# Start of a fused mLSTM and SwiGLU kernel: weight halves on two DMA queues, output gates asked for first, weight block 0 scaled later

## The chip, the cores and the metric

The kernel runs on one NeuronCore of one Trainium2 chip. The metric is the device time of one execution in microseconds (us); lower is better. Beside the plain times there is one profiled execution, whose trace says when each instruction of each engine ran. The engines are PE (matmul, with PEld for its weight loads), DVE (vector), ACT (scalar and activation), POOL (GpSimd) and SP, which only issues DMAs. ACT can issue DMAs too. Each engine works through its own list of instructions in order and waits at an instruction until the semaphores that it names have been raised.

## The reference

First comes an mLSTM cell over 4 batches x 8 heads, 768 steps, head size 40. For each step:

```python
m_new = np.maximum(f_gate[:, :, t] + m, i_gate[:, :, t])
f_stab = np.exp(f_gate[:, :, t] + m - m_new)
i_stab = np.exp(i_gate[:, :, t] - m_new)
C = f_stab * C + i_stab * (v_t outer k_t)
n = f_stab * n + i_stab * k_t
o = 1.0 / (1.0 + np.exp(-o_gate[:, :, t]))
y[:, :, t] = o * (C q_t) / np.maximum(np.abs(n . q_t), 1.0)
```

Its result, seen as x with 3072 tokens and 320 columns (8 heads x 40), goes through a SwiGLU block with 1536 hidden columns:

```python
g = x @ w_gate
val = x @ w_val
out = (g * sigmoid(g) * val) @ w_out
```

q, k, v and the gates are float32. The weights are float64 in memory, so each weight arrives as two 32-bit words.

## The kernel before, in words

The 768 steps are cut into six groups of 128. Group g covers 4 batches x 128 steps, 512 tokens. For each group the cell gives x, a *seam* turns x on PE into xT, and the SwiGLU block runs over 12 blocks m of 128 hidden columns. `hidden(g, m)` does the 10 matmuls gv_ps of both projections (20 in the trace[...]), SiLU on ACT and the product on DVE; `project` multiplies with w_out. While PE does the blocks of group g, the steps of the cell for group g + 1 are put between them by hand in lists called `slots` and `after`. The order on each engine is that of the program text (`manual_schedule`).

Group 0 is special: nothing runs ahead of it. The code from `burn(7)` to `late_sums()` is this start. The cell of group 0 is done in one square of 128 steps, in halves of two batches:

- `first_turn`, `first_scores`, `first_own`, `first_x`: transposes, scores, products and the division that gives x without the output gate.
- `sig(P)`: the sigmoid of the output gates o_sb of half P, on ACT.
- `first_gate(P)`: x times the output gate on DVE; POOL copies 64 columns.
- `first_seam(P, engs)`: 10 transposes on PE in three PSUM tiles (four, four and two transposes), copied to xT by the engines in `engs`; A is ACT, V is DVE.
- `first_state(P, eng)`: the state at the end of the group.
- `burn(n)`: n matmuls on junk data.

Weights come in *pieces*. `PIECES` lists them: pieces 0 and 1 hold one block of w_gate and w_val, pieces 2 to 6 two blocks each, pieces 7 to 9 four blocks of w_out. Piece p from 2 to 6 thus holds blocks 2p - 2 and 2p - 1. A piece of gate and val has two halves, the w_gate half on partitions 0 to 63 and the w_val half on 64 to 127; a half of two blocks is 640 KB. `piece_load(p, home, second)` asks for the w_gate half on SP and for the w_val half on the queue `second` (ACT unless told otherwise). The raw words go into one of two `raw` buffers or into a `home`: piece 2 and later piece 6 lie in h_sb, piece 3 in wo_sb.

A block is then turned from float64 words to float32 in three steps: `scale(j)` on ACT makes `top` and `low` (L184, L186), `join(j)` on DVE puts the top bits together (L193, L194), `rounded(j)` adds `low`, on POOL unless another engine is named (L201). `convert(j)` does all three. In group 0 `hidden(0, m)` converts block m + 2 after its own matmuls and before its own SiLU.

f_sb and i_sb hold the gate rows of the later steps (80 KB each); `late_sums`, `late_maxima`, `late_turns` and `decay` work on them during group 0.

DMAs are told apart by eight semaphores that are dealt out in turn to the DMAs of both queues. A DMA whose semaphore is already in use waits, on the engine that issues it, until the earlier DMA on that semaphore has landed. Whatever stands behind it on that engine waits too.

Of the kernel before, what the change touches and what calls it, by code (L numbers as in the profile page):

```python
# [18 lines left out]
L = 128  # L19
# [5 lines left out]
def kernel(  # L25
# [18 lines left out]
    nc = tc.nc  # L44
# [12 lines left out]
    NKC = DM // HP  # L57
    UH = BH // 2
    UA = UH // 2
    NH = NFC + 1  # L60
# [12 lines left out]
    def flat(t):  # L73
        return t.rearrange("p c t -> p (c t)")

    def bank(name, tag="cell"):
        return psum.tile([128, 512], F32, name=name, tag=tag)
# [4 lines left out]
    def heads(P):  # L82
        return slice(P * UH, (P + 1) * UH)
# [4 lines left out]
    o_sb = const.tile([128, BH, D], F32)  # L88
# [8 lines left out]
    wo_sb = const.tile([128, NFC, DM], F32)  # L97
    h_sb = const.tile([128, NH, TW], F32)
# [7 lines left out]
    f_sb = early.tile([BH, NS - 2, SUB], F32)  # L106
    i_sb = early.tile([BH, NS - 2, SUB], F32)

    def tokens(a, c, P):
        return a[2 * P:2 * P + 2, :, ts(c, L), :].rearrange("b h p d -> p (b h) d")  # L110

    def load(dst, a, c, P):
        nc.sync.dma_start(out=dst[:, heads(P), 0:D], in_=tokens(a, c, P))

    def copy(eng, dst, src):
        if eng is nc.scalar:
            nc.scalar.copy(dst, src)
        else:
            eng.tensor_copy(dst, src)

    def gate_rows(a):
        return a.rearrange("b h s -> (b h) s")

    def spread_rows(a):
        return gate_rows(a)[:, 0:L].unsqueeze(0).to_broadcast([128 // BH, BH, L])

    nc.scalar.dma_start(out=f0, in_=spread_rows(f_gate))
    nc.sync.dma_start(out=i0, in_=spread_rows(i_gate))


    raws = {}
    PIECES = [("gv", 0, 1), ("gv", 1, 1)] + [("gv", m, 2) for m in range(2, NFC, 2)] + [("o", m, 4) for m in range(0, NFC, 4)]

    def piece_load(p, home=None, second=nc.scalar):
        kind, m, n = PIECES[p]
        if kind == "gv":
            a, d = NKC, n * 128
            src = [(slice(i * HP, (i + 1) * HP), w[:, m * 128:(m + n) * 128].rearrange("(c p) f -> p c f", p=HP))
                   for i, w in enumerate((moe_w_gate, moe_w_val))]
            queues = (nc.sync, second)  # L140
        else:
            a, d = n, DM
            src = [(slice(0, 128), moe_w_out[m * 128:(m + n) * 128].rearrange("(a p) d -> p a d", p=128))]
            queues = (nc.sync,)
        if src[0][1].dtype == F32:
            for r, w in src:
                if kind == "o":
                    nc.sync.dma_start(out=wo_sb[r, m:m + n, :], in_=w)
                else:
                    for x in range(n):  # L150
                        nc.sync.dma_start(out=wgv_sb[r, m + x], in_=w[:, :, ts(x, 128)])
            return
        if home is None:
            raw = conv.tile([128, 4 * NKC * 128], U32, name="raw")
        else:
            raw = home.rearrange("p a t -> p (a t)").bitcast(U32)
        raw = raw[:, 0:2 * a * d]
        for (r, w), queue in zip(src, queues):
            queue.dma_start(out=raw[r].rearrange("p (a d) -> p a d", a=a), in_=w.bitcast(U32))
        words = raw.rearrange("p (a d two) -> p a d two", two=2, a=a)  # L160
        raws[p] = (words[:, :, :, 0], words[:, :, :, 1])
        split(p)
# [4 lines left out]
    def split(p):  # L167
        if p in raws:
            lo, hi = raws.pop(p)
            kind, m, n = PIECES[p]  # L170
            if kind == "gv":
                for c in range(n):
                    r = slice(c * 128, (c + 1) * 128)
                    blocks[m + c] = (lo[:, :, r], hi[:, :, r], wgv_sb[:, m + c])
            else:
                for c in range(0, n, 2):
                    blocks[NFC + (m + c) // 2] = (lo[:, c:c + 2], hi[:, c:c + 2], wo_sb[:, m + c:m + c + 2, :])

    def scale(j):
        if j in blocks:  # L180
            lo, hi, dst = blocks[j]
            a, d = hi.shape[1], hi.shape[2]
            top = conv.tile([128, NKC * 128], F32, name="top", bufs=1).rearrange("p (a d) -> p a d", a=a)
            nc.scalar.mul(top, hi.bitcast(F32), 2.0 ** -112)  # L184
            low = conv.tile([128, NKC * 128], I32, name="low").rearrange("p (a d) -> p a d", a=a)
            nc.scalar.mul(low, lo, 2.0 ** -29)  # L186
            blocks[j] = (low, top.bitcast(U32), dst)

    def join(j):
        if j in blocks:  # L190
            lo, top, dst = blocks[j]
            both = dst.bitcast(U32)
            nc.vector.tensor_scalar(both, top, scalar1=3, scalar2=None, op0=ALU.logical_shift_left)  # L193
            nc.vector.scalar_tensor_tensor(both, in0=top, scalar=0x80000000, in1=both, op0=ALU.bitwise_and,  # L194
                                           op1=ALU.bitwise_or)
            blocks[j] = (lo, dst.bitcast(I32))

    def rounded(j, eng=None):
        if j in blocks:
            lo, dst = blocks.pop(j)  # L200
            (eng or nc.gpsimd).tensor_tensor(dst, dst, lo, op=ALU.add)  # L201
# [198 lines left out]
    def xT(n):  # L400
        return xTs[max(n - 1, 0) % 2]
# [32 lines left out]
    def sig(P):  # L434
        nc.scalar.activation(o_sb[:, heads(P)], o_sb[:, heads(P)], AF.Sigmoid)


    def burn(n, tag="cell"):
        t = bank("burn", tag)
        for _ in range(n):  # L440
            nc.tensor.matmul(t, lhsT=junk[:, 0:128], rhs=junk, start=True, stop=True)  # L441
# [4 lines left out]
    A, V, G = nc.scalar, nc.vector, nc.gpsimd  # L446
# [29 lines left out]
    def first_turn(P, src, dst, engs):  # L476
        for b in range(2):
            tp = bank("tp_kq").rearrange("p (a t) -> p a t", t=L)
            for a in range(UA // 2):
                h = P * UH + b * H + 2 * a  # L480
                nc.tensor.transpose(tp[:, a, :], src[:, h:h + 2, :].rearrange("p h d -> p (h d)"), ident)  # L481
            a = P * UA + b * UA // 2
            copy(engs[b], dst[:, a:a + UA // 2, :], tp)
# [20 lines left out]
    def first_x(u):  # L504
        y = first_y.pop(u)
        den = work.tile([128, UH, 1], F32, name="den")[:, 0:H]
        nc.vector.tensor_scalar(den, y[:, :, D:], scalar1=1.0, scalar2=None, op0=ALU.max)
        nc.vector.scalar_tensor_tensor(den, in0=y[:, :, D:], scalar=-1.0, in1=den, op0=ALU.mult, op1=ALU.max)
        nc.vector.reciprocal(den, den)
        nc.vector.tensor_tensor(x_sb[:, u, 0:DM].rearrange("p (h d) -> p h d", d=D), y[:, :, 0:D],  # L510
                                den.to_broadcast([128, H, D]), op=ALU.mult)

    def first_gate(P):
        for u in (2 * P, 2 * P + 1):
            x = x_sb[:, u, 0:DM].rearrange("p (h d) -> p h d", d=D)
            nc.vector.tensor_tensor(x, x, o_sb[:, u * H:(u + 1) * H], op=ALU.mult)
        nc.gpsimd.tensor_copy(x_sb[:, 2 * P:2 * P + 2, DM:], x_sb[:, 2 * P:2 * P + 2, 0:HP])
# [9 lines left out]
    def first_seam(P, engs):  # L527
        for c, eng in zip(range(0, NKC, 2), engs):
            cs = range(c, min(c + 2, NKC))
            tp = bank("tp_x")[:, 0:len(cs) * 2 * L].rearrange("p (c u s) -> p c u s", u=2, s=L)  # L530
            for w in cs:
                for b in range(2):
                    nc.tensor.transpose(tp[:, w - c, b, :], x_sb[:, 2 * P + b, ds(PAIRS[w][0] * HP, 2 * HP)], ident)
            copy(eng, xT(0)[:, c:c + len(cs), 2 * P * L:(2 * P + 2) * L].rearrange("p c (u s) -> p c u s", u=2), tp)
# [13 lines left out]
    first_turn(1, k_sb, kT, (A, A))  # L548
    first_x(0)
    first_turn(1, q_sb, qT, (A, V))  # L550
    piece_load(0)
    load(o_sb, o_gate, 0, 1)
    piece_load(1)
    first_own(1)
    first_values(1)
    first_x(1)
    first_scores(1)
    sig(0)
    nc.scalar.dma_start(out=flat(f_sb), in_=gate_rows(f_gate)[:, L:])
    nc.scalar.dma_start(out=flat(i_sb), in_=gate_rows(i_gate)[:, L:])  # L560
    piece_load(2, h_sb[:, NH - NKC:], nc.sync)
    piece_load(3, wo_sb, nc.sync)
    scale(0)
    sig(1)
    burn(3)
    first_own(2)
    first_own(3)
    first_gate(0)
    first_x(2)
    join(0)  # L570
    first_x(3)
    rounded(0)
    first_gate(1)
    first_seam(0, (A, V, A))
    burn(8, "gen")
    piece_load(4)
    first_seam(1, (V, A, A))
    first_state(0, A)
    convert(1)
    piece_load(5)  # L580
# [222 lines left out]
```

## Time and profile before

| what | value |
|---|---|
| median of 3 runs | 576.04 us (573.17 to 576.25) |
| the profiled execution's own time | 576.29 us |
| its span, first to last instruction | 574.5 us |
| mean granted PE clock | 0.994 |
| moved by DMA | 39.82 MB in 168220 packets |

The profiled execution is 1.8 us longer than its span: that lies before the first and after the last instruction. The page gives the busy time of each engine, then the span in 40 slices. In the slices a digit is the busy share in tenths:

```
PEclk 9989899999999999999999999999999999999999
DMA  9999993396265530355450264360000000000000
```

Each slice is 14.4 us. The granted PE clock dips in the third and the fifth, and the DMA engines are full in the first six.

### The profile page before, as it was taken

The page shows a single profiled execution, that of the slowest core. Times are in us where ns is not written, and L with a number is a line of the kernel's source. Part 1 is how long each engine was busy: PE and PEld are TensorE (multiplying, and loading weights), DVE is VectorE, ACT ScalarE, POOL GpSimd, SP SyncE. Part 2 cuts the span into 40 slices and gives each one's busy share as a digit, 9 for nine tenths or more (in the row PEclk, how much of TensorE's full clock was granted, in tenths as well). Part 3 has the DMA queues.
Part 4 walks back from the last instruction along what each step waited for, and adds up shares of the span by engine and source line. Part 5 has one row for each costly group of instructions (what it writes and reads, how often), then busy time and mean ns, then how long its engine had stood idle before and what let it go on. Part 6 is the DMA issues. An engine that isn't in the chain of part 4 may idle for free.

```text
span 574.5 us, 11872 instructions
## 1 busy us (share of the span) xinstructions
PE 561.7 (98%) x5216; PEld 326.3 (57%) x5218; DVE 219.7 (38%) x378; ACT 143.7 (25%) x224; POOL 107.6 (19%) x104
## 2 busy tenths in 40 slices
PE   9979899999999999999999999999999999999997
PEld 4844545666555566455567455567455567544475
DVE  5656568781335620424630433640333730011100
ACT  4345556433410114210114211024211010111100
POOL 2122425555301132001232001232001110000000
PEclk9989899999999999999999999999999999999999
DMA  9999993396265530355450264360000000000000
GB/s 124 179 208 187 175 264 66 116 167 114 28 68 71 98 57 23 46 60 63 79 86 23 34 71 49 65 111 25 13 2 2 2 2 23 24 1 1 0 24 23
DMA packets 168220, 39.82 MB, mean 69 GB/s; under 512 B 158728, under 2 KB 163336, under 8 KB 168168
## 3 DMA queue, kind: packets, MB, share of 16 engines
q1 hardware_dynamic: 166260, 36.20, 39.5%
q10 hardware_dynamic: 1908, 2.85, 2.6%
q8 instruction: 41, 0.67, 0.5%
q14 instruction: 11, 0.09, 0.0%
HBM read 35.03 MB, written 4.01 MB: 68 GB/s over the span
## 4 chain that ended last, share of the span: by engine, by line
PE 87%; DMA 6%; DVE 3%; ACT 2%; POOL 1%; issue 1%; SPq 0%; ACTq 0%; DVEq 0%; POOLq 0%
PE gv_ps L618 48%; PE o_ps L634 23%; PE o_ps L641 4%; DMA wo_sb<-in_moe_w_val_dram 4%; DMA raw<-in_moe_w_gate_dram 2%; PE intra L370 2%; PE inter L365 2%; PE sp L325 1%; PE add L346 1%; PE tp_x L411 1%; PE burn L441 1%; PE first_y L502 1%; DVE wgv_sb L194 1%; PE tp_kq L481 1%; DVE wgv_sb L193 1%
## 5 line engine op out<-in xcount | busy, mean ns | idle before, releaser
L618 PE MATMUL gv_ps<-xT,wgv_sb 64*128 64x512 f32 x1440 | 321.5, 596 | 3.9 <-POOL wgv_sb L201 3.4
L618 PEld LDWEIGHTS gv_ps<-xT,wgv_sb 64*128 64x128 f32 x1440 | 140.5, 188 | 160.0 <-issue 152.0
L624 DVE TENSOR_TENSOR h_sb<-sg,gv_ps 128x512 f32<-128x512 f32 x72 | 49.5, 687 | 288.3 <-ACT sg L623 273.0
L634 PE MATMUL o_ps<-wo_sb,h_sb 128*128 128x320 f32 x480 | 130.5, 433 | 0.0
L634 PEld LDWEIGHTS o_ps<-wo_sb,h_sb 128*128 128x128 f32 x480 | 90.8, 190 | 38.2 <-issue 0.8
L623 ACT ACTIVATE sg<-gv_ps 128x512 f32<-128x512 f32 x72 | 43.0, 597 | 262.4 <-PE gv_ps L618 262.4
L355 POOL TENSOR_TENSOR C<-C,dec 128x328 f32<-128x328 f32 x20 | 14.5, 737 | 150.3 <-DVE C L357 150.3
L628 ACT COPY z_sb<-o_ps 128x320 f32<-128x320 f32 x24 | 10.2, 426 | 114.1 <-PE o_ps L634 102.7
L428 POOL TENSOR_SCALAR_AFFINE_SELECT w_sb<-w_sb 64x1024 f32<-64x1024 f32 x20 | 28.2, 1408 | 26.1 <-DVE w_sb L423 25.1
L641 PE MATMUL o_ps<-wo_sb,h_sb 128*128 128x320 f32 x96 | 26.9, 437 | 0.0
L391 POOL TENSOR_TENSOR o_sb<-o_sb,y_sb 128x640 f32<-128x640 f32 x10 | 14.2, 1428 | 48.4 <-DVE y_sb L382 48.4
L641 PEld LDWEIGHTS o_ps<-wo_sb,h_sb 128*128 128x128 f32 x96 | 17.9, 190 | 7.2
L201 POOL TENSOR_TENSOR wgv_sb<-wgv_sb,low 128x640 int32<-128x640 int32 x9 | 14.9, 1654 | 33.8 <-DVE wgv_sb L194 30.0
L382 DVE TENSOR_TENSOR y_sb<-y_sb,intra 64x328 f32<-64x328 f32 x40 | 19.7, 493 | 0.9
L335 POOL TENSOR_TENSOR vw_sb<-v_sb,w_sb 128x656 f32<-128x656 f32 x10 | 12.9, 1316 | 31.3 <-issue 29.4
L365 PEld LDWEIGHTS inter<-C,qT 64*64 64x64 f32 x640 | 10.2, 134 | 7.3 <-issue 6.1
L193 DVE TENSOR_SCALAR wgv_sb<-top 128x640 uint32<-128x640 uint32 x12 | 9.0, 746 | 13.0 <-ACT top L184 13.0
L357 DVE TENSOR_TENSOR C<-C,add 128x328 f32<-128x328 f32 x20 | 9.9, 493 | 10.5 <-POOL C L355 10.5
L184 ACT ACTIVATE top<-raw 128x640 f32<-128x640 f32 x12 | 9.6, 799 | 14.1 <-issue 5.3
L423 DVE TENSOR_TENSOR w_sb<-g_T,w_sb 128x1024 f32<-128x1024 f32 x10 | 13.1, 1350 | 0.0
L201 POOL TENSOR_TENSOR wo_sb<-wo_sb,low 128x640 int32<-128x640 int32 x6 | 10.2, 1707 | 15.0 <-DVE wo_sb L194 10.5
L332 DVE TENSOR_TENSOR w_sb<-sp,w_sb 128x512 f32<-128x512 f32 x20 | 12.7, 681 | 0.0
(126 smaller groups left out, 378.3 us busy)
## 6 DMA issues: line engine op xcount, KB each, us to landing
w_sb<-M_dram SPq DMA_DIRECT2D x10, 512.0 KB, 6.4
k_sb<-in_k_dram SPq DMA_DIRECT2D x12, 320.0 KB, 5.7
v_sb<-in_v_dram SPq DMA_DIRECT2D x12, 320.0 KB, 7.2
o_sb<-in_o_gate_dram SPq DMA_DIRECT2D x12, 320.0 KB, 7.0
raw<-in_moe_w_out_dram SPq DMA_DIRECT2D x3, 1280.0 KB, 7.5
out_dram<-z_sb SPq DMA_DIRECT2D x24, 160.0 KB, 1.8
q_sb<-in_q_dram SPq DMA_DIRECT2D x6, 320.0 KB, 8.2
q_sb<-in_q_dram SPq DMA_DIRECT2D x24, 64.0 KB, 2.3
```

The source lines that it names most:

```text
L193: nc.vector.tensor_scalar(both, top, scalar1=3, scalar2=None, op0=ALU.logical_shift_left)
L201: (eng or nc.gpsimd).tensor_tensor(dst, dst, lo, op=ALU.add)
L355: nc.gpsimd.tensor_tensor(state(s + 1)[:, a], state(s)[:, a], dec[:, s - 2, a].unsqueeze(2).to_broadcast([128, UA, D1]), op=ALU.mult)
L365: nc.tensor.matmul(inter[two][half(i), a, :], lhsT=qT[half(two), P * UA + a, half(i)], rhs=state(2 * n + i)[half(two), P * UA + a, :], sta ...
L382: nc.vector.tensor_tensor(t, t, intra[i][half(c)], op=ALU.add)
L391: eng.tensor_tensor(o, o, y[:, :, 0:D], op=ALU.mult)
L428: nc.gpsimd.affine_select(w, w, compare_op=ALU.is_ge, fill=NEG, base=0, pattern=[[0, UH], [1, SUB]], channel_multiplier=-1)
L618: nc.tensor.matmul(ps[i], lhsT=wgv_sb[half(i), m, PAIRS[kc][i], :], rhs=x[half(i), kc, :], start=(kc == 0), stop=(kc == NKC - 1))
L623: nc.scalar.activation(sg, ps[0], AF.Silu)
L624: nc.vector.tensor_tensor(hid(g, m), sg, ps[1], op=ALU.mult)
L634: nc.tensor.matmul(p, lhsT=hid(g, m)[:, ts(u, L)], rhs=wo_sb[:, m, :], start=(m == 0), stop=(m == NFC - 1))
L641: nc.tensor.matmul(ps[u], lhsT=hid(g, m)[:, ts(u, L)], rhs=wo_sb[:, m, :], start=(m == 0), stop=(m == NFC - 1))
```

## The change

Four edits, all in the start of group 0:

1. The requests for f_sb and i_sb move from behind `sig(0)` to the very start, right behind the first gate loads, on ACT.
2. The output gates of half 1 are asked for ahead of piece 0.
3. The val halves of pieces 2 and 3 are asked for on ACT, not on SP; both sigmoids stand ahead of these requests.
4. `scale(0)`, `join(0)` and `rounded(0)` move back. Scaling stands behind ACT's two copies of the first seam, joining behind the gating of half 1 (and behind `piece_load(4)` in the text), rounding behind the copies of the second seam, and on DVE instead of POOL. The third copy of each seam, the small one, goes to DVE and the first two to ACT. The second burn has 6 matmuls instead of 8.

```diff
     nc.sync.dma_start(out=i0, in_=spread_rows(i_gate))
+    nc.scalar.dma_start(out=flat(f_sb), in_=gate_rows(f_gate)[:, L:])
+    nc.scalar.dma_start(out=flat(i_sb), in_=gate_rows(i_gate)[:, L:])
...
-    def piece_load(p, home=None, second=nc.scalar):
+    def piece_load(p, home=None):
...
-            queues = (nc.sync, second)
+            queues = (nc.sync, nc.scalar)
...
     first_turn(1, q_sb, qT, (A, V))
+    load(o_sb, o_gate, 0, 1)
     piece_load(0)
-    load(o_sb, o_gate, 0, 1)
     piece_load(1)
     first_own(1)
     first_values(1)
     first_x(1)
     first_scores(1)
     sig(0)
-    nc.scalar.dma_start(out=flat(f_sb), in_=gate_rows(f_gate)[:, L:])
-    nc.scalar.dma_start(out=flat(i_sb), in_=gate_rows(i_gate)[:, L:])
-    piece_load(2, h_sb[:, NH - NKC:], nc.sync)
-    piece_load(3, wo_sb, nc.sync)
-    scale(0)
     sig(1)
+    piece_load(2, h_sb[:, NH - NKC:])
+    piece_load(3, wo_sb)
     burn(3)
     first_own(2)
     first_own(3)
     first_gate(0)
     first_x(2)
+    first_x(3)
+    first_seam(0, (A, A, V))
+    scale(0)
+    first_gate(1)
+    burn(6, "gen")
+    piece_load(4)
     join(0)
-    first_x(3)
-    rounded(0)
-    first_gate(1)
-    first_seam(0, (A, V, A))
-    burn(8, "gen")
-    piece_load(4)
-    first_seam(1, (V, A, A))
+    first_seam(1, (A, A, V))
+    rounded(0, V)
     first_state(0, A)
     convert(1)
     piece_load(5)
```

Where a line number is given for the changed kernel, the added lines shift it: L184, L186, L193, L194 and L201 become L186, L188, L195, L196 and L203.

## The prediction

> **What bounds the kernel now.** I read the page first, then the windows, then the timelines of PE and ACT, then the chain of waits.
>
> ```profile
> span 574.5 us, 11872 instructions
> ...
> PE 561.7 (98%) x5216; PEld 326.3 (57%) x5218; DVE 219.7 (38%) x378; ACT 143.7 (25%) x224; POOL 107.6 (19%) x104
> ```
>
> TensorE is busy for 98% of the span, so time can come only from where it waits, or from work at a lower clock. The PE timeline (start, length, engine, line, tiles, and in brackets the idle time before) shows where:
>
> ```profile
> 31.99 2.31 PE L533 MATMUL tp_x<-ident,x_sb 128*128 128x128 f32 x10 [2.60 <-DVE x_sb L516]
> ...
> 36.10 4.91 PE L618 MATMUL gv_ps<-xT,wgv_sb 64*128 64x512 f32 x20
> ...
> 43.57 13.15 PE L618 MATMUL gv_ps<-xT,wgv_sb 64*128 64x512 f32 x60 [1.50 <-POOL wgv_sb L201]
> ...
> 59.32 6.50 PE L618 MATMUL gv_ps<-xT,wgv_sb 64*128 64x512 f32 x20 [1.88 <-POOL wgv_sb L201]
> ```
>
> The reader is to see three waits: 2.60 us for gated x, 1.50 for weight block 1, 1.88 for block 4. The last group takes 6.50 us where others take 4.4 (13.15 / 3). The windows say why (columns: stretch, length, busy us of PE, PEld, DVE, ACT and POOL, granted PE clock, DMA share, GB/s):
>
> ```profile
> 36.00:43.00 7.00, 6.00 (x56) 2.79 (x54) 3.50 (x4) 4.02 (x7) 2.07 (x1) 0.99 1.06 207
> 44.00:50.00 6.00, 6.00 (x30) 2.71 (x28) 5.31 (x10) 4.51 (x7) 2.98 (x3) 1.00 1.06 208
> ...
> 60.00:63.45 3.45, 3.45 (x11) 2.71 (x9) 3.42 (x7) 2.10 (x4) 1.55 (x1) 0.51 1.55 141
> ```
>
> After the wait the clock is halved up to 63.45 us. The first two lines show the DMA engines full (share over 1) at 207 and 208 GB/s. Now ACT, in the stretch that leads to block 4:
>
> ```profile
> 40.82 0.61 ACTq L159 DMA_DIRECT2D raw<-in_moe_w_val_dram  x1
> ...
> 52.60 0.73 ACT L279 ACTIVATE keep<-keep 32x640 f32<-32x640 f32 x1 [2.54 <-DVE keep L278]
> 54.77 0.60 ACTq L159 DMA_DIRECT2D h_sb<-in_moe_w_val_dram  x1
> 55.42 0.79 ACT L184 ACTIVATE top<-wo_sb 128x640 f32<-128x640 f32 x1 [2.09 <-DMA raw<-in_moe_w_gate_dram]
> ```
>
> Block 4 belongs to piece 3, whose halves landed at 40.8 and 43.9 (requests at 22.98 and 23.68, 17.8 and 20.2 us to landing). Yet ACT scales it at 55.42. Ahead of it in ACT's order stands the request for piece 6's val half, at 54.77, and this waits for the landing of piece 5's val half, because both use one of eight DMA semaphores: 40.82 + 13.9 = 54.7. From there to PE the chain of waits is fixed:
>
> ```profile
> 55.44 0.77 ACT top L184
> ...
> 57.73 1.54 POOL wgv_sb L201
> 59.28 0.04 issue
> 59.32 6.50 PE gv_ps L618 x20
> ```
>
> So PE's restart at 59.32 is the landing of piece 5's val half (54.7) plus 4.6 us. The page's chain names another transfer there (piece 5's gate half), but that landed at 43.95 + 12.6 = 56.6, after ACT had gone on, so it cannot be the releaser.
>
> [...] 207 GB/s where nearly all packets are SP's (36 to 43 us), 208 where nearly all are ACT's (44 to 50). [...] from 30 to 34 us: 248 packets of SP's queue, 252 of ACT's. [...] nearly all of piece 5's val half had moved by 51 us, but it counted as landed at 54.7. [...] The two halved stretches (clock 0.51 in 32.7 to 36.1 and 60.0 to 63.45) are 27.3 us apart[...].
>
> **The change part by part, up to block 0.**
> - *Gate rows f_sb, i_sb first.* Two requests (0.37 + 0.32 us) stand ahead of ACT's table load at 1.92; ACT then idles 6.07 us, which hides them. Their 160 KB take 0.8 us of DMA at 202 GB/s, ahead of k, q, v. Cover: k lands at 7.1 and is read at 10.26, q at 9.4 against 11.19; the second k, q at 13.9 and 16.2 against 16.65 and 17.56. Uncovered it would cost 0 to 0.5 us, all before block 4. Later, 0.69 us of requests and their waits leave ACT (the second request waited to 27.38).
> - *Output gates ahead of piece 0.* ACT's request for piece 1's val half no longer waits for piece 0's gate half (4.08 us idle before L435). Sigmoid of half 0 starts near 21.5 (copy ends 18.9, two requests of 0.65, table 1.28) instead of 24.25. Then DVE is the limit: L495 ends at 23.98, so the gating starts there instead of at 25.02.
> - *Block 0 moved behind.* On DVE: gating 0.89 to 24.9; two first_x of 1.12, the last from 26.55 (PE's L502 end) to 27.7; the small copy 0.4 (estimate, half of 0.69); gating of half 1 0.89 (1.47 before, beside POOL's L201) to 29.0. PE's second turn follows its burn (27.5 + 6 x 0.25 = 29.0), so it starts at 29.0 instead of 31.99. Turn 1.29, state 1.0 (1.94 at half clock): 31.3. ACT copies to 28.3, scales block 0 to 29.8; DVE joins (0.50 + 0.83) to 30.5, copies to 30.9, rounds in 0.8 (row L201 on DVE at 80.41) to 31.8. POOL loses one L201 of 1.53.
> - So block 0's matmuls start at 31.8 instead of 36.10. Two fewer burn matmuls are covered by that.
> - *Blocks 1 to 3.* Piece 1 (requested from 18.9 on) is down before 30; block 1 is ready at 35.7, PE wants it at 31.8 + 4.4 + 1.0 = 37.2. Piece 2's halves share the engines and land near 37 (36.8 before); block 2 is ready at about 41.4, wanted at 41.6. Both waits go. PE is through block 3 and tp_g at 31.8 + 4.4 + 1.0 + 13.1 + 0.8 = 51.1 instead of 57.4: 6.3 us ahead.
>
> **What is late next: block 4.** The order of instructions built from the changed kernel has the request for piece 6's val half still ahead of block 4 on ACT, still on the semaphore of piece 5's val half. Behind it on ACT stand top and low of block 4 and the SiLU of block 2; DVE, POOL and PE wait for those. So all depends on when piece 5's val half lands. It is asked for at about 36.8 (after piece 2's gate half landed) instead of 40.82. But the bytes ahead of it are the same: all of k, q, v, o, the gate rows, pieces 0 to 4. From 20 to 54 us the DMA engines ran full, at 202 to 208 GB/s; an earlier request only queues longer.
> - Lower bound of the landing: 53.7. From 18 to 20 us the engines ran at share 0.53 and 111 GB/s (200 elsewhere), a hole of about 0.9 us that the earlier ACT requests can fill.
> - Upper bound of the likely case: 56.6. Piece 5's gate half, requested at about 43, shares by packet with the val half instead of following it; then both end when the later one ended before.
> - I take the middle, 55.2, so PE restarts at 55.2 + 4.6 = 59.8 instead of 59.3. By 63.45, still at half clock, it does (63.45 - 59.8) / 2 = 1.83 us of its 4.4, against 2.07 before: 0.24 us lost. The 6.3 us won turn into a wait of 8.7 us for block 4.
>
> After block 4 the order of every engine is unchanged, and k, q of the next group queue behind the same bytes (the earliest, q, landed at 65.8 and is read at 71.1). Sum against the profiled execution, 576.29 us: 576.29 + 0.2 = 576.5. The runs shown have a median of 576.04, 0.25 below that execution.
>
> **Rivals.**
> - *Faster: the request carries.* If ACT's own queue lets piece 5's val half land 4 us earlier, as it is asked for, at 50.7: PE restarts at 55.3, loses 1.7 to one halved window, ends block 4 at 61.4 instead of 65.8: 571.9. With no wait at all it ends at 55.5: 566.0. For it: the two early waits do go, and ACT's requests no longer wait behind scaling. Against it: DMA share above 1 throughout.
> - *Slower: the wait grows.* Place: ACT's request for piece 6. With two full queues the val half of piece 5 shares with its gate half and then with the next k. Landing at 58.5, PE restarts at 63.1, [...]the clock stays halved to 66.9, block 4 ends at 69.4: 3.6 us later, 579.9. It decides from a landing of 57.1 on (restart 61.7, 2.9 us lost). Against it: the k request is small and behind both halves.
> - *The change doesn't do what it says*: the built order shows each request on its new queue and place, so I give it no share of its own.
>
> **How the numbers follow.** No change is the likeliest: landing between 53.7 and 56.6, restart 58.3 to 61.2, time 575.8 to 577.2 (up to 578.9 if the clock stays halved a window longer). A measurement of this kernel can tell about 0.5%, 2.9 us, from no change. I give the forecast 0.56. Faster 0.28, since my landing rests on a ledger of bytes[...]. Slower 0.16. The range leaves out about 0.1 at either end: 569.0 to 580.0.
>
> **What would show it.** Right: gv_ps first at about 32; no wait at L618 for block 1; one wait of 6 to 10 us at L618 near 51 to 60, released through POOL L201 (now L203); ACT idle before its top<-wo_sb, right behind the request of piece 6; DMA share near 1.05 up to 54. Wrong: top<-wo_sb before 52, or that wait below 4 us; then the order of transfers, not their sum, set the end. Wrong at the start: gv_ps first at 35 or later.

## The result: 0.6% faster, and the profile after

The changed kernel takes 572.26 us (median of 9 runs, 570.04 to 572.64) against 576.02 for the kernel before on the same chip (9 runs, 573.17 to 576.4). The ratio is 0.9942, interval 0.9922 to 0.9962. In a second set of runs it was 571.82 (17 runs, 569.41 to 575.59) against 574.29, ratio 0.9957 (0.9938 to 0.9976). The medians thus differ by 3.8 and by 2.5 us. The forecast was no change, 576.5.

The profiled execution took 572.01 us, 4.28 less than that of before. That is more than the medians differ by, since the profiled execution of before, 576.29, is among the longest of that kernel. From the page: the span, the busy times, and the DMA engines in 40 slices of 14.3 us (their busy share in tenths, then the rate).

```profile
span 570.2 us, 11868 instructions
...
PE 559.7 (98%) x5215; PEld 328.4 (58%) x5216; DVE 219.5 (38%) x379; ACT 144.3 (25%) x224; POOL 106.1 (19%) x103
...
DMA  9999991593472810454630355450000000000000
GB/s 124 179 271 193 173 265 45 134 146 82 48 83 36 140 28 25 46 67 53 109 48 23 49 58 66 77 85 23 13 2 2 2 1 34 13 0 1 0 24 23
```

In the third slice (28.5 to 42.8 us) the DMA engines are as busy as ever, a 9, and move 271 GB/s; in the kernel before, the same slice had a 9 and 208:

```profile
GB/s 124 179 208 187 175 264 66 116 167 114 28 68 71 98 57 23 46 60 63 79 86 23 34 71 49 65 111 25 13 2 2 2 2 23 24 1 1 0 24 23
```

Now PE's timeline of the kernel after (start, length, engine, line, tiles, idle time before in brackets):

```profile
29.03 1.42 PE L535 MATMUL tp_x<-ident,x_sb 128*128 128x128 f32 x10
31.93 4.56 PE L618 MATMUL gv_ps<-xT,wgv_sb 64*128 64x512 f32 x20 [0.43 <-DVE wgv_sb L203]
37.49 13.54 PE L618 MATMUL gv_ps<-xT,wgv_sb 64*128 64x512 f32 x60
54.63 6.50 PE L618 MATMUL gv_ps<-xT,wgv_sb 64*128 64x512 f32 x20 [2.87 <-POOL wgv_sb L203]
```

The waits for x and for block 1 are gone. Block 4 still waits, 2.87 us, and still runs for 3.4 us at half clock (6.50 in all), but it starts 4.69 us earlier than the 59.32 of before. Its end moves from 65.82 to 61.13, also 4.69 us; that is the whole gain of the profiled execution (4.28) and a little more. ACT's timeline and the chain of waits (start, length, what) show what it waits for:

```profile
47.90 0.73 ACT L281 ACTIVATE keep<-keep 32x640 f32<-32x640 f32 x1 [3.01 <-DVE keep L280]
50.02 0.60 ACTq L161 DMA_DIRECT2D h_sb<-in_moe_w_val_dram  x1
50.73 0.79 ACT L186 ACTIVATE top<-wo_sb 128x640 f32<-128x640 f32 x1 [2.09 <-DMA raw<-in_moe_w_val_dram]
```

```profile
33.48 16.46 DMA raw<-in_moe_w_val_dram
...
50.02 0.60 ACTq L161
...
50.73 0.80 ACT top L186
...
53.05 1.54 POOL wgv_sb L203
...
54.63 6.50 PE gv_ps L618 x20
```

ACT's request for piece 6 stands ahead of block 4's scaling as before and waits for piece 5's val half, as before. That half is asked for at 33.48 and lands at 49.95; before, 40.82 and 54.7. So the landing moved by 4.7 us, and the windows (stretch, length, busy us of PE, PEld, DVE, ACT, POOL, granted clock, DMA share, GB/s) say how:

```profile
26.00:32.00 6.00, 5.57 (x67) 4.42 (x66) 4.82 (x12) 4.01 (x9) 0.30 (x1) 1.00 1.12 201
33.00:39.00 6.00, 6.00 (x58) 3.25 (x56) 4.80 (x7) 1.45 (x3) 3.14 (x2) 1.00 1.04 351
40.00:43.00 3.00, 3.00 (x15) 1.58 (x13) 1.40 (x4) 2.99 (x6) 1.55 (x1) 1.00 1.06 198
44.50:47.00 2.50, 2.50 (x14) 2.18 (x12) 2.50 (x3) 0.39 (x1) 0.98 (x1) 1.00 1.06 338
```

The share in the column before last is 1.04 to 1.12 throughout, and the rate jumps between 200 and 350. At a share of 1.05 the rate was not at a ceiling.

### The profile page after: what moved, and what is told of

Read it like the earlier page. It is cut to its first block, busy times and chain, and to the rows that moved or that the text cites. A ratio compares the mean times of both kernels' runs of the same rounds, so it can differ in the third digit from the quotient of the medians.

```text
span 570.2 us, 11868 instructions
## 1 busy us (share of the span) xinstructions
PE 559.7 (98%) x5215; PEld 328.4 (58%) x5216; DVE 219.5 (38%) x379; ACT 144.3 (25%) x224; POOL 106.1 (19%) x103
## 4 chain that ended last, share of the span: by engine, by line
PE 84%; DMA 5%; SPq 3%; ACT 3%; DVE 3%; POOL 1%; issue 1%; ACTq 0%; DVEq 0%; POOLq 0%
PE gv_ps L618 49%; PE o_ps L634 23%; PE o_ps L641 4%; SPq L113 3%; DMA raw<-in_moe_w_val_dram 3%; PE intra L372 2%; PE inter L367 2%; DMA raw<-in_moe_w_gate_dram 2%; PE sp L327 1%; PE add L348 1%; PE tp_x L413 1%; DVE wgv_sb L196 1%; DVE wgv_sb L195 1%; POOL C L357 1%; PE tp_kq L292 0%
## 5 line engine op out<-in xcount | busy, mean ns | idle before, releaser
L618 PEld LDWEIGHTS gv_ps<-xT,wgv_sb 64*128 64x128 f32 x1440 | 144.2, 188 | 156.3 <-issue 148.1
L634 PEld LDWEIGHTS o_ps<-wo_sb,h_sb 128*128 128x128 f32 x480 | 90.8, 190 | 38.2 <-issue 0.8
L203 POOL TENSOR_TENSOR wgv_sb<-wgv_sb,low 128x640 int32<-128x640 int32 x8 | 13.3, 1668 | 28.5 <-DVE wgv_sb L196 28.5
L203 POOL TENSOR_TENSOR wo_sb<-wo_sb,low 128x640 int32<-128x640 int32 x6 | 10.2, 1708 | 15.0 <-DVE wo_sb L196 10.5
L372 PE MATMUL intra<-v_sb,w_sb 64*64 64x41 f32 x640 | 12.3, 228 | 0.4 <-DVE C L359 0.3
L186 ACT ACTIVATE top<-raw 128x640 f32<-128x640 f32 x12 | 9.6, 800 | 11.5 <-issue 5.3
```

The lines of the kernel that those rows point to most:

```text
L372: nc.tensor.matmul(intra[i][half(c), a, :], lhsT=w_sb[half(i), h, :], rhs=v_sb[half(i), h, :], start=True, stop=True)
L618: nc.tensor.matmul(ps[i], lhsT=wgv_sb[half(i), m, PAIRS[kc][i], :], rhs=x[half(i), kc, :], start=(kc == 0), stop=(kc == NKC - 1))
L634: nc.tensor.matmul(p, lhsT=hid(g, m)[:, ts(u, L)], rhs=wo_sb[:, m, :], start=(m == 0), stop=(m == NFC - 1))
```

## The experiments

A half of two blocks is 640 KB, 320 packets of 2 KB. Counting packets by queue in each trace shows which halves are in flight when. A packet carries no name, so 320 are counted off to each half in the order of the requests. The bounds are rough: a few packets of a half come late, and piece 3's val half, counted full at 39.5 us in the kernel after, landed at 42.5. In the kernel after, SP moves the gate halves of pieces 2 to 5 in 27.8 to 31.5, 31.5 to 35.6, 35.7 to 41.0 and 43.8 to 48.7 us; ACT moves the val halves in 32.4 to 36.3, 36.4 to 39.5, 39.6 to 42.9 and 42.9 to 48.8. So in 33 to 39 and in 44.5 to 47 a gate half (partitions 0 to 63) and a val half (64 to 127) move together; in 40 to 43 val halves move almost alone (5 packets of SP). In the kernel before, the halves that met were two val halves (piece 2 on SP, piece 1 on ACT).

**Theory 1:** a half fills only one side of the partitions and gets about 200 GB/s, however many queues carry halves of that side; two halves of opposite sides move at about 350. **Rivals:** any two queues double the rate; or two source tensors do; or the gain comes from the earlier requests and from block 0's early start at an unchanged rate.

**Pieces 2 and 3 on one queue.** In the kernel after:

```diff
-    piece_load(2, h_sb[:, NH - NKC:])
-    piece_load(3, wo_sb)
+    piece_load(2, h_sb[:, NH - NKC:], (nc.sync, nc.sync))
+    piece_load(3, wo_sb, (nc.sync, nc.sync))
```

> The changed kernel, but pieces 2 and 3 ask for both halves on SP, as before. T1 (a half fills one side of the partitions, a gate half and a val half in flight together move at about twice the rate of one): in the stretch where pieces 2 and 3 move the DMA rate stays near 205 GB/s, piece 5's val half lands at 53 to 55 instead of 50.0, block 4's matmuls start near 58.5 and the time goes back to 574.5 to 576.5. T3 (the gain comes from the earlier requests and the moved steps alone, at one rate): landing near 50, time near 572.

Measured: 573.47 us (22 runs), 0.9976 of before (0.9962 to 0.999). Two stretches of its windows:

```profile
38.00:42.00 4.00, 0.24 (x2) 0.24 (x4) 3.93 (x4) 3.20 (x5) 2.87 (x2) 1.00 1.06 201
46.00:48.00 2.00, 2.00 (x12) 0.92 (x10) 0.68 (x1) 0.00 (x0) 1.18 (x1) 1.00 1.06 346
```

From 38 to 42 us both queues are at work, 197 packets of SP and 195 of ACT, and together they move 201 GB/s: the val half of piece 3 on SP, that of piece 4 on ACT. From 46 on, gate halves on SP meet a val half on ACT: 346. Piece 1's val half, which also met a val half, landed at 36.72, and PE waited 3.92 us for block 1; block 4 then had no wait. So with these two pieces on one queue the other edits keep about half of the gain (0.24% of 0.43 to 0.58%); the intervals of this run and of the kernel after touch or overlap, so the share is an estimate. I had not reckoned with the later pairs: piece 5's val half landed at 52.25.

**The queues alone.** In the kernel before:

```diff
-    piece_load(2, h_sb[:, NH - NKC:], nc.sync)
-    piece_load(3, wo_sb, nc.sync)
+    piece_load(2, h_sb[:, NH - NKC:])
+    piece_load(3, wo_sb)
```

> The kernel before, but the val halves of pieces 2 and 3 are asked for on ACT; nothing else is moved. T1: about 340 GB/s or more for some 6 us, piece 5's val half lands near 50 to 51, block 4 no longer waits; the start of block 0 is not earlier than 36 us, so block 3 ends near 57 to 58, and the time is 572 to 573.5. T3: DMA rate near 205 GB/s, landing near 54.7, block 4 at 59.3, time near 576.

Measured: 575.15 us (14 runs), 1.0011 (0.9997 to 1.0024). The rate came for a while, the time did not. Two stretches of the windows, and ACT's timeline:

```profile
32.50:36.00 3.50, 1.59 (x7) 1.38 (x8) 3.04 (x7) 0.44 (x2) 1.74 (x2) 0.79 1.03 350
36.00:41.00 5.00, 4.40 (x45) 2.71 (x43) 0.39 (x1) 0.49 (x2) 0.00 (x0) 0.81 1.06 209
```

```profile
39.87 0.60 ACTq L159 DMA_DIRECT2D raw<-in_moe_w_val_dram  x1
40.51 0.86 ACT L117 COPY xT<-tp_x 128x512 f32<-128x512 f32 x2 [7.58 <-DMA wo_sb<-in_moe_w_gate_dram]
```

In the old order of the program ACT stands 7.58 us at piece 4's request, which waits for a landing, and the copy of xT stands behind it. Block 0 starts at 38.41 (36.10 before), and piece 5's val half is asked for at 43.10 and lands at 54.66. The pair itself broke up at 36 us, though halves of opposite sides were asked for on both queues: from 36 to 38 ACT moved 193 packets and SP 22, from 38 to 41 SP moved 277 and ACT 43, at 209 GB/s. So requests on two queues were not enough here: the rate fell from 350 to 209 GB/s when one of them hardly moved.

**Piece 2 on SP, piece 3 on ACT.** In the kernel after:

```diff
-    piece_load(2, h_sb[:, NH - NKC:])
-    piece_load(3, wo_sb)
+    piece_load(2, h_sb[:, NH - NKC:], (nc.sync, nc.sync))
+    piece_load(3, wo_sb, (nc.scalar, nc.scalar))
```

> The changed kernel, but piece 2 has both halves on SP and piece 3 both on ACT, so two queues are in use, with two gate halves (partitions 0 to 63) in flight together, then two val halves (64 to 127). T1: near 205 GB/s in that stretch although both queues move packets, landing of piece 5's val half 53 to 55, time 574.5 to 576.5. T2 (any two queues double the rate): near 350 GB/s, landing near 50, time near 572.

Measured: 572.91 us (22 runs), 0.9961 (0.9947 to 0.9976), and 327 GB/s from 33 to 38.5:

```profile
33.00:38.50 5.50, 5.22 (x46) 2.73 (x44) 4.37 (x5) 1.79 (x3) 2.44 (x1) 1.00 1.05 327
```

The meeting that was meant did not take place: SP was one half ahead, so that piece 2's val half met piece 3's gate half, and then piece 4's gate half met piece 3's val half. The run says only that the halves of one piece need not meet each other, as long as sides do.

**The same with ACT's halves exchanged**, so that the same sides meet:

```diff
-        for (r, w), queue in zip(src, queues):
+        for (r, w), queue in zip(src[::turn], queues):   # turn is -1 for piece 3
```

> The kernel after, with piece 2 wholly on SP's queue (gate half, then val half) and piece 3 wholly on ACT's queue with its val half first. SP's queue is about one half ahead, so from 35 us on SP carries the val half of piece 2 and ACT the val half of piece 3: two queues at once, but both into partitions 64 to 127. In the run before it, with ACT's order gate first, opposite halves met there, and 33 to 39 us went at 329 GB/s. Theory 1 (opposite partitions make the rate): where the two val halves meet, about 200 GB/s, piece 2's val half down near 41 and not 38.9, piece 5's val half later than 52.3, 574 to 577 us. Rival (any two queues at once make the rate): about 330 GB/s in 35 to 39, the same landings as there, 573 us.

Measured: 576.6 us (8 runs), 1.0038 (1.0019 to 1.0056), slower than before. Its windows:

```profile
35.00:38.00 3.00, 3.00 (x12) 1.46 (x10) 2.60 (x3) 1.02 (x2) 1.13 (x1) 0.57 1.06 197
40.00:42.00 2.00, 2.00 (x38) 1.30 (x36) 0.27 (x3) 0.00 (x0) 0.01 (x1) 1.00 1.06 198
42.00:45.00 3.00, 3.00 (x16) 1.35 (x16) 1.32 (x2) 2.22 (x3) 0.00 (x0) 1.00 1.06 259
```

The meeting of val halves that was meant hardly took place. Most of piece 2's val half had moved alone on SP before 35 us, and from 35 to 38 ACT moved 276 packets, most of them of piece 3's val half, beside 29 of SP, at 197 GB/s. From 40 to 42 gate meets gate, 103 packets of SP and 90 of ACT: 198. From 42 to 45 a gate and a val half are in flight, with about as many packets of each queue, at 259: more than one side gives, less than the 327 to 351 of the other windows. Why it is less is not shown. Nothing but the order of two requests on ACT differs from the run before it. Together with the two val halves of 38 to 42 us above (201 GB/s) this says that any two queues do not double the rate; opposite sides raise it.

**Another source.** In the kernel after, the second half of pieces 2 to 6 comes from w_gate:

```diff
-            src = [(slice(i * HP, (i + 1) * HP), w[:, m * 128:(m + n) * 128]...
-                   for i, w in enumerate((moe_w_gate, moe_w_val))]
+            cols = (m, (m + 6) % NFC if n == 2 else m)
+            src = [(slice(i * HP, (i + 1) * HP), w[:, cols[i] * 128:(cols[i] + n) * 128]...
+                   for i, w in enumerate((moe_w_gate, moe_w_gate if n == 2 else moe_w_val))]
```

> The kernel after, with one thing changed: the second half of pieces 2 to 6 (the half that goes to partitions 64 to 127 on ACT's queue) is read from w_gate, six blocks further on, and not from w_val; sizes, queues, partitions and order stay. So half of those weights are not the reference's. Theory 1 (the rate depends on which partitions the two transfers in flight write): nothing changes, 33 to 39 us at about 350 GB/s, piece 5's second half down near 50, PE restarts for block 4 at 54 to 55, 572 to 573 us. Rival (the rate depends on the two source tensors lying apart in device memory): both halves now come from one tensor, 33 to 39 us at about 205 GB/s, piece 5's second half down at 53.7 to 56.6, 575 to 577 us.

Measured: 572.72 us (11 runs; a twelfth took 578.0), 0.997 (0.9948 to 0.9991).

```profile
33.00:39.00 6.00, 6.00 (x56) 3.24 (x54) 4.84 (x7) 1.48 (x3) 3.15 (x2) 1.00 1.05 349
```

Both halves from one tensor: 349 GB/s as well. The source tensor is out as the cause. ACT's request for piece 6 stood at 51.80, not near 50, so the landing was later than theory 1 had it.

**The kernel after once more**, beside these:

> The kernel after, unchanged, beside the other versions on one chip, to set the after without its queue edit (0.9976 of before) against it. Theory 1 (the queues' halves on opposite partitions give the rate): 0.994, about 571.3 us, so that some 0.35% of the gain is the queue edit's on top of the other two. Rival (the queues give nothing, the other two edits give all): 0.9976, about 573.3.

Measured: 571.82 us, 0.9957 (0.9938 to 0.9976), nearer to theory 1's number than to the rival's, which lies at the end of the interval. Its profiled execution was one of the long ones, 575.28 us, and shows one thing that can make the same kernel long:

```profile
33.00:38.00 5.00, 4.72 (x28) 2.35 (x29) 3.91 (x5) 1.81 (x4) 2.35 (x1) 1.00 1.06 229
39.00:43.00 4.00, 4.00 (x20) 1.68 (x20) 1.37 (x3) 3.09 (x4) 0.80 (x1) 1.00 1.07 336
```

From 35 to 38 us SP moved 6 to 15 packets per us where ACT moved 87 to 97. By the count these are the last 40 or so of piece 3's gate half, asked for at 24 us; piece 4's, asked for at 31.8, begins only near 38. With one queue standing there is no pair; piece 6's request came at 52.71 and block 4 at 57.31. Block 4 then took 7.17 us, for the clock was halved for 6.8 us (55.55 to 62.38). What makes a queue stand I could not settle.

**Block 0 put back.** In the kernel after, with all its requests:

```diff
+    scale(0)
     burn(3)
...
     first_x(2)
+    join(0)
     first_x(3)
-    first_seam(0, (A, A, V))
-    scale(0)
+    rounded(0)
     first_gate(1)
-    burn(6, "gen")
+    first_seam(0, (A, V, A))
+    burn(8, "gen")
     piece_load(4)
-    join(0)
-    first_seam(1, (A, A, V))
-    rounded(0, V)
+    first_seam(1, (V, A, A))
```

> The kernel after, with block 0's scaling, joining and rounding put back to where the kernel before has them (and that seam's copies and 8 burn matmuls), all requests of the change kept. If the landing of piece 5's val half sets block 4, block 0 some 3 to 4 us later (gv_ps first at 35 to 36) costs little: ACT asks for pieces 4 and 5 later (near 34 and 38), but the bytes ahead of them still move as pairs, the val half lands at 50 to 52, PE restarts for block 4 at 55 to 57 with a shorter wait: 571 to 573.5 us, ratio 0.994 to 0.998. Rival (the early start of block 0 is what brings the gain): PE is late from block 0 on, 574.5 to 576 us, ratio 1.0.

Measured: 571.03 us (6 runs), 0.9929 (0.9911 to 0.9948), no worse than the kernel after. PE's timeline:

```profile
36.18 5.54 PE L618 MATMUL gv_ps<-xT,wgv_sb 64*128 64x512 f32 x20
42.72 13.15 PE L618 MATMUL gv_ps<-xT,wgv_sb 64*128 64x512 f32 x60
56.53 4.56 PE L618 MATMUL gv_ps<-xT,wgv_sb 64*128 64x512 f32 x20
```

Block 0 starts at 36.18, as late as before the change, yet block 4 ends at 61.09, where the kernel after ends it at 61.13. PE comes to block 4 at 56.5, when its weights are there; block 4 has no wait and no half clock. (The clock was halved earlier, from 31.4 to 38.2, when block 0 took 5.54 us.) So the early start of block 0 was turned into a wait, as the forecast said; the gain comes with the requests and their transfers, which this run keeps.

**Piece 6 asked for later.** In the kernel after:

```diff
-        1: [run(late_maxima), run(piece_load, 6, h_sb[:, NH - NKC:])],
-        2: [run(weights_load, 1), ...
+        1: [run(late_maxima)],
+        2: [run(piece_load, 6, h_sb[:, NH - NKC:]), run(weights_load, 1), ...
```

> The changed kernel with the load of piece 6 moved from the end of slot 1 to the head of slot 2, so that on ACT the scaling of block 4 and the SiLU of block 2 stand ahead of piece 6's request. If that request's wait is what holds block 4 (piece 3 landed at 42.5): no wait for block 4, no halved clock, PE goes on at 51.8, 2.9 us of wait and 2.1 us of half clock less, time near 567.2. If block 4 is held by its own landing or by conversion: no change, near 572.

Measured: 568.39 us (6 runs, 567.76 to 570.14), 0.9894 (0.987 to 0.9919). It beats both kernels. PE's timeline:

```profile
37.49 13.26 PE L618 MATMUL gv_ps<-xT,wgv_sb 64*128 64x512 f32 x60
52.16 4.80 PE L618 MATMUL gv_ps<-xT,wgv_sb 64*128 64x512 f32 x20 [0.67 <-POOL wgv_sb L203]
```

The window around it:

```profile
50.00:57.00 7.00, 6.33 (x35) 4.33 (x32) 5.67 (x13) 5.31 (x8) 3.08 (x2) 1.00 1.11 153
```

With the request behind block 4 the wait shrinks from 2.87 to 0.67 us and the clock stays up (1.00 in the window). The request for piece 6 is the holder of block 4.

**The same move in the kernel before:**

> The kernel before, with one thing changed: the load of piece 6 is asked for at the head of slot 2 and no longer in slot 1, so its request stands behind block 4's scaling on ACT and not ahead of it. If the request for piece 6, waiting for piece 5's val half, holds block 4 in the kernel before as it does after: piece 3 was down at 43.9, so block 4 is scaled by 50 and PE goes on at 57.4 without wait and at full clock, ends block 4 at 62.0 and not 65.8: 3.8 us less, about 571 us on this chip (before 574.6), ratio 0.993. Rival (block 4 is held by something else, SiLU or the joins on DVE): no change, 574 to 575.5.

Measured: 572.38 us (22 runs), 0.9965 (0.9955 to 0.9975): about half of what was expected. PE's timeline:

```profile
37.92 2.85 PE L618 MATMUL gv_ps<-xT,wgv_sb 64*128 64x512 f32 x12 [1.81 <-ACT xT L117]
43.32 14.84 PE L618 MATMUL gv_ps<-xT,wgv_sb 64*128 64x512 f32 x60 [1.49 <-POOL wgv_sb L201]
58.83 4.56 PE L618 MATMUL gv_ps<-xT,wgv_sb 64*128 64x512 f32 x20
```

The stretch in which the clock was halved:

```profile
43.67:47.09 3.42, 3.42 (x10) 1.39 (x8) 3.07 (x7) 2.09 (x4) 1.70 (x2) 0.50 1.07 213
```

Block 4's wait is gone here too, so the request holds block 4 in the kernel before as well. But in this execution part of blocks 1 to 3 ran at half clock, after the waits of 1.81 and 1.49 us: 14.84 us where 13.15 was. These 1.7 us kept block 4 to 58.8 instead of 57.4. The profiled execution, 573.81, is one of the longer ones; whether the same thing holds back the median is not shown.

**Piece 6 later, with pieces 2 and 3 on one queue:**

> The version with piece 6 in slot 2, with both halves of pieces 2 and 3 on SP's queue. It says what the queues are worth once piece 6's request no longer stands ahead of block 4. If the pairing of halves sets when weights are there: the val halves of pieces 1 and 2 meet again, block 1 waits 3 to 4 us as in the earlier run with these two pieces on one queue, which had no wait at block 4, so nothing more is won: 572.5 to 574 us, ratio 0.997, against 0.989 with both queues. Rival (with piece 6 out of the way the queues no longer matter): 568.5 us, ratio 0.989.

Measured: 572.46 us (6 runs), 0.9949 (0.993 to 0.9969). With both queues the same version has 0.9894, so the pairing is worth about 0.55% here (each ratio is to the kernel before on the same chip). It shows at block 1, where the val halves of pieces 1 and 2 meet again:

```profile
42.26 14.68 PE L617 MATMUL gv_ps<-xT,wgv_sb 64*128 64x512 f32 x60 [3.64 <-POOL wgv_sb L202]
```

## Why the prediction was wrong

**The start: right.** Gating from 24.13 us (forecast 24), PE's second turn at 29.03 (29.0), block 0 at 31.93 (31.8), no waits at blocks 1 and 2, the end of block 3 and tp_g (the small transposes of the gates, L592) at 51.76 (51.1). The cover of the moved gate rows held: PE turned the first k at 9.96 and the last q at 17.76, 0.2 us later than before.

**The holder of block 4: right.** The same distance from ACT's request for piece 6 to PE's restart is found wherever block 4 waited long:

| kernel | request for piece 6 | block 4 starts | difference | profiled time |
|---|---|---|---|---|
| before | 54.77 | 59.32 | 4.55 | 576.29 |
| after | 50.02 | 54.63 | 4.61 | 572.01 |
| after, once more | 52.71 | 57.31 | 4.60 | 575.28 |
| another source | 51.80 | 56.40 | 4.60 | 573.51 |
| piece 2 on SP, 3 on ACT | 52.38 | 56.97 | 4.59 | 574.35 |
| the same sides met | 55.66 | 60.29 | 4.63 | 578.68 |

**The landing: wrong, and this is the step that failed.** "From 20 to 54 us the DMA engines ran full, at 202 to 208 GB/s; an earlier request only queues longer." From this came a landing of piece 5's val half at 55.2, not before 53.7; it was 49.95. Its request stood at 33.48, earlier than the 36.8 of the forecast, but the bytes ahead of it were indeed the same. But the share of busy DMA engines was read as a ceiling of the rate, and here it was none (351 GB/s at a share of 1.04, 207 at 1.06): 6 us at 351 instead of 207 GB/s spare 6 x 144 / 207 = 4.2 us, 2.5 us at 338 another 1.6. These 5.7 us are an estimate; 4.7 show in the landing, and where the other 1.0 went I have not shown. The sum then fails by this one term: forecast 576.5, with the landing 5.2 us too late; block 4's end 66.0 where 61.13 was measured, the time 4.5 above the profiled execution. Two of the forecast's own signs of being wrong came, the scaling of block 4 at 50.73 (before 52) and the wait of 2.87 us (below 4). One of its signs of being right, a DMA share near 1.05, came as well: the share did not tell the two cases apart.

The trace of before held the warning, in a stretch that the forecast does not use. There w_out's pieces arrive, on all 128 partitions and on one queue, in packets of 2.5 KB, at a share no higher than that of the 207 GB/s:

```profile
82.00:86.00 4.00, 4.00 (x20) 1.75 (x18) 3.88 (x4) 1.45 (x3) 1.99 (x1) 1.00 1.03 411
30.00:34.00 4.00, 1.93 (x10) 1.60 (x10) 3.54 (x7) 0.59 (x2) 1.82 (x2) 0.84 1.09 196
```

The first line is one queue on both sides of the partitions, the second two queues on one side. The stretches that the forecast has beside its one rate are of one queue that moved nearly alone (207 and 208 GB/s) or of two that both wrote one side (248 and 252 packets from 30 to 34 us, at 196 GB/s); none of them shows what two queues on opposite sides do. The runs do: 198 GB/s where val halves moved almost alone, 351 where opposite halves moved together. They show that the side of the partitions decides, and that the source tensor (349 with both halves from one) and the number of queues (201 with two queues on one side) do not. Why the side decides is not shown.

**The rivals.** "The request carries" had nearly the right numbers (landing 50.7, restart 55.3, 571.9) by half of the mechanism: it knew of early requests and not of sides, so that its numbers came so near is in part luck. Early requests with pieces 2 and 3 on one queue give 0.9976, two queues with the old requests 1.0011, both together 0.9942 and 0.9957. The wait that grows did not come with this change; it came in the run where the same sides met, with a request at 55.66 and 576.6 us.

**The half clock** was priced as if it held from PE's restart to 63.45 us, with 1.83 us of block 4 done by then for a restart at 59.8. The trace of before has it from 60.04 to 63.45, 0.7 us after the restart, and that of after from 55.80, 1.2 us after the restart:

```profile
55.80:59.21 3.41, 3.41 (x10) 2.65 (x8) 3.34 (x7) 1.62 (x3) 1.54 (x1) 0.50 1.30 120
```

Block 4 took 6.50 us in both, 1.9 more than the 4.56 of the same block where it ran at full clock (block 0 put back). So the price was the same as before the change, and the forecast's 0.24 us of extra loss was not there. The slower rival's clock, halved until 66.9 us, was the author's estimate: that a later restart prolongs the half clock is not shown.

## What to carry to other kernels

Before a transfer is called bound by bandwidth, look for the highest rate at the same DMA share anywhere in the trace: here 411 beside 207 GB/s. Tensors that fill half of the partitions each are worth loading so that opposite halves are in flight together (351 against 198 GB/s here), here by two queues with requests early enough on both. Both queues must really move at once, which the requests alone did not ensure (209 GB/s with the queues alone). And ask which instruction stands behind a DMA request that waits: moving one request by one slot took the kernel after from 0.9942 and 0.9957 to 0.9894 of before, about as much again as the whole change, and the kernel before to 0.9965.

## What was not expected of the hardware

- Two queues writing the same side share about 200 GB/s (201 with pieces 2 and 3 on one queue, 198 where the same sides met); writing opposite sides they move 327 to 351 while both have as many packets (259 in one stretch), at the same DMA share of 1.03 to 1.06. A packet of 2 KB takes about half as long in a pair. In the kernel after, the microsecond from 40 us has 98 such packets at a share of 1.04, 16 x 1.04 us / 98 = 170 ns each; that from 38 us has 187 at 1.05, 90 ns each.
- A queue stood while its transfer had long been asked for. In the kernel after, piece 4's gate half was all but through at 39.5 us, its last packets came up to 41.0, and piece 5's, asked for at 37.7, moved nothing before 43.8. From 35 to 38 us of the second profile SP moved 6 to 15 packets per us, and with the queues alone SP and ACT took turns from 36 to 41. Such a gap cost the pair (199 GB/s from 41.0 to 43.8 us of the kernel after); between the two profiles of the same kernel piece 6's request differs by 2.7 us (52.71 against 50.02), of which the gap is the likely cause. What causes the gap stays open.
- Four of the waits were paid for twice, and the second price didn't follow the first. After 2.87 us block 4 lost 1.9 us to the halved clock (6.50 against 4.56), after 3.68 us (the kernel after once more) 2.6 (7.17), and after 3.92 and 3.64 us (pieces 2 and 3 on one queue, without and with piece 6 later) blocks 1 to 3 lost 1.7 and 1.5 (14.84 and 14.68 against 13.15). In these traces the clock stays halved for 3.4 us (55.80 to 59.21 in the kernel after) or for twice that (55.55 to 62.38 in the second profile), and the loss is about half of the time that PE worked in it: 3.41 us there, 5.07 here.
